# Two moves in a two-layer spectral MLP: GpSimd issues the stores of a matrix's sums, and VectorE adds a seventh product earlier

## The chip, the core and the metric

The kernel runs on one core of a Trainium2 chip. The engines of the core work side by side, each through its own list of instructions in order: TensorE (PE in the profile; PEld is its loading of weights) multiplies into the banks of PSUM, VectorE (DVE) and ScalarE (ACT) work elementwise, GpSimd (POOL) does small elementwise work here, and SyncE (SP; its queue is SPq) issues the transfers between the device's memory and the on-chip memory SBUF. An instruction that waits for a semaphore holds up everything behind it in its engine's list. The metric is the device time of one execution in microseconds; less is better.

## What is computed

Two sublayers, A and B, run in turn, twice, over one sequence of 2048 rows with 512 features, all in float32.

```python
# A: Fourier mixing, the real part of a DFT over rows and features
a = einsum("bsd,ed->bse", x, dft_hid_re);  b = einsum("bsd,ed->bse", x, dft_hid_im)
y = einsum("ts,bse->bte", dft_seq_re, a) - einsum("ts,bse->bte", dft_seq_im, b)
# B: a shift between rows, then an MLP with 1376 hidden features
h  = gelu(layernorm(x) @ w1);  x1 = x + shifted(h) @ w2
out = x1 + gelu(layernorm(x1) @ w3) @ w4
# the whole
x = x + A(layernorm(x));  x = x + B(layernorm(x))     # layer 0
x = x + A(layernorm(x));  x = x + B(layernorm(x))     # layer 1
```

## The kernel before

**Numbers in two parts.** Every operand of a product is split into a high part (a rounded copy, made by ScalarE) and a low part (what the copy lost, made by VectorE). A product is then three matmuls (`mm3`, lines 343 to 345): high by high, high by low, low by high.

**Sublayer A by chunks.** The 2048 output rows are four chunks of 512. In each chunk an x phase (`x_phase`) and a y phase (`y_phase`) multiply the coefficients of the DFT over rows with sums and differences of the input's rows. Each phase runs over eight pairs of row tiles. The x phase accumulates into the PSUM banks psc, psb and psa, the y phase into psc, psd, psb and psa. The coefficients come from memory into the buffers `raw`, and are split into a ring of four slots, `ring0` to `ring3`: VectorE forms a difference (line 285), ScalarE casts it (286), VectorE makes the low part (300). `stream()` hands out the next slot, and before it does, it prepares as many later ones as the ring has room for; so each `stream()` in the code is also a place where VectorE, ScalarE and SyncE get work.

**The product with the hidden DFT matrix.** The 512x512 product of a chunk with the DFT over features is made of seven smaller products of half-sized blocks instead of eight, the seven forms. In layer 1 the x phase of a chunk also multiplies the seven forms of the chunk before it. `HAT7 = (5, 10, 11, 12, 13, 14, 15)` gives the step of the x phase, two to a pair of tiles, at which each form is multiplied (`hid7`, into psd, two banks in turn). One step later VectorE adds its result into the rows X1 or pairs[1] (`hid7_out`, line 520, a `tmp<-tmp,psd` at line 567). The seventh form falls on step 15, the last, so its add has no step behind it: it comes after the last product of the x phase (line 616), behind whatever the last `stream()`, the late work and the hook of step 15 have put into VectorE's list: the low part of a sum of w4's blocks (line 1883), and in chunks 1 and 2 the statistics of two row tiles (lines 377 to 382).

**The right forms.** The seven right-hand blocks of the hidden DFT matrix, each in high and low part, are made once, in layer 0, and kept in memory as `hsd`. That happens beside the last pair of chunks of layer 0's MLP, in four quarters (`hs_forms`, `hs_quarter`): a quarter loads two blocks `hs` of the matrix (lines 1208 and 1211), VectorE forms four sums, and then, in four steps, ScalarE casts (line 1224), VectorE makes the low parts (1229) and the result is stored (1230). Three buffers `hp` (hp0, hp1 and hp2) serve the seven stores of a quarter, so hp1 is used three times and hp0 and hp2 twice. Each step rides with one step of preparing layer 1's input (`bg`), among them the statistics of row tiles, whose power and product run on GpSimd (lines 362 and 363). The MLP's own transfers go through the same queue of SyncE: `w4r` (line 943) and `w3b` (line 958) are the weights of the products that TensorE runs meanwhile. The products of the MLP go through four banks, psa and psd, which VectorE empties by adds named `rest<-rest,psa` and `rest<-rest,psd` (line 567).

The order on each engine is the order in which the Python code issues instructions; no scheduler moves them.

Of the kernel before, what the change touches and what calls it, by code (L numbers as in the profile page):

```python
# [8 lines left out]
F32 = mybir.dt.float32  # L9
# [9 lines left out]
NP = NT // 2  # L19
# [26 lines left out]
def spectral_mlp_kernel(ctx: ExitStack, tc: tile.TileContext, x, ws, hs, w1, w2, w34, out):  # L46
    nc = tc.nc
# [110 lines left out]
    def piece(src, a=0, b=2):  # L158
        pieces.append((src, a, b))
        return len(pieces) - 1  # L160
# [25 lines left out]
    for layer in range(LAYERS):  # L186
        for c in range(NC):
# [15 lines left out]
            for k in range(NP):  # L203
# [4 lines left out]
                p = piece(ws[c, k][:, 2:4])  # L208
# [120 lines left out]
    def stream():  # L329
        i = state["use"]  # L330
        if i and items[i - 1][3] is None:
            state["done"] += 1
        state.update(use=i + 1, over=i)
        prefetch()
        while state["two"] <= i:
            stage_two()
        if items[i][0] == "form":
            return raw_in[place[items[i][1][0]]]
        return slots.pop(i)


    def mm3(o, lh, ll, rh, rl, first, last, more=False):
        nc.tensor.matmul(o, lh, rh, start=first, stop=False, skip_group_check=more)  # L343
        nc.tensor.matmul(o, lh, rl, start=False, stop=False, skip_group_check=more)  # L344
        nc.tensor.matmul(o, ll, rh, start=False, stop=last, skip_group_check=more)  # L345
# [153 lines left out]
    def hid7(n):  # L499
        ps, (lo, _) = PD[n % 2], forms[n]  # L500
        new = n in (0, 1, 3, 6)
        for h in range(2):
            s = stream()
            for i in range(2):
                j = 2 * h + i
                for q in range(2):
                    v = slice(q * P, (q + 1) * P)
                    first = new and not (j or q)
                    o = ps[:, q * DH : (q + 1) * DH]
                    mm3(o, hf[n % 2][:, j, v], lo[:, j, v], s[:, i, 0], s[:, i, 1], first, True, not first)  # L510

    def hid7_out(n):
        ps = PD[n % 2].rearrange("p (t d) -> p t d", t=2)
        x1, x2 = X1, pairs[1]
        if n == 4:
            x2 = x2.rearrange("p t (h d) -> p t h d", h=2)
            add(x2, x2, ps.unsqueeze(2).broadcast_to([P, 2, 2, DH]))
            return
        t, v = ((x1, left), (x2, left), (x1, right), (x2, right), None, (x1, right), (x1, left))[n]
        add(t[:, :, v], t[:, :, v], ps, ALU.subtract if n == 1 else ALU.add)  # L520
# [45 lines left out]
    def add(o, a, b, op=ALU.add):  # L566
        nc.vector.tensor_tensor(o, a, b, op=op)  # L567

    def run_late(*names):
        for i in names:  # L570
            for f in late.pop(i, ()):
                f()

    def x_phase(c, hook, seven=False, tiles=0):
        h = 0
        re0s, re1s, im0s, im1s = by_tile[tiles]
        ready = []

        def form_steps(step):
            if seven and step in HAT7:  # L580
                ready.append(HAT7.index(step))
                hid7(ready[-1])

        def form_outs(step):
            while ready and HAT7[ready[0]] < step:
                hid7_out(ready.pop(0))

        for k in range(NP):
            first, last = k == 0, k == NP - 1
            form_steps(2 * k)  # L590
            while c and not seven and h < NP and HAT[h] == k:
                s = stream()
                ri, dp = HORDER[h % 4]
                hid(ri, dp, s, PD, 2 * (h // 4), h % 4 == 0, h % 4 == 3)
                if h % 4 == 3:
                    at_mix = c == NC - 1 and h > 4
                    add_y(c - 1, h // 4, PD, X1, "10" if at_mix else 2 * k if h < 4 else "y", xs[5] if at_mix else X1)
                h += 1
            s = stream()
            run_late(2 * k)  # L600
            hook(2 * k)
            form_outs(2 * k)
            mm_half(PC, ax[k][:, 2], s[:, 0], first, last)
            mm_half(PB, ax[k][:, 1], s[:, 1], first, last)
            form_steps(2 * k + 1)
            if last:
                for i in range(2):
                    nc.scalar.copy(im1s[:, i], PC[i])  # L608
                for i in range(2):
                    nc.scalar.copy(re1s[:, i], PB[i])  # L610
            s = stream()
            run_late(2 * k + 1)
            hook(2 * k + 1)
            form_outs(2 * k + 1)
            mm_half(PA, ax[k][:, 0], s[:, 0], first, last)
        form_outs(2 * NP)
        for i in range(2):
            nc.scalar.copy(re0s[:, i], PA[i])
# [78 lines left out]
    def hid(ri, dp, s, acc, t0, first, last):  # L697
        for i in range(2):
            for t, a in enumerate(acc):
                w = slice((t0 + t) * P, (t0 + t + 1) * P)  # L700
                mm3(
                    a,
                    rr[ri][dp][:, i, 0, w],
                    rr[ri][dp][:, i, 1, w],
                    s[:, i, 0],
                    s[:, i, 1],
                    first and i == 0,
                    last and i == 1,
                )
# [3 lines left out]
    def add_y(c, half, ps, to, defer, kept=None):  # L713
        j = c * TC + 2 * half
        for i in range(2):
            add(to[:, i], ps[i], to[:, i])
        late.setdefault(defer, []).append(lambda: y_stats(j, to if kept is None else kept))
# [140 lines left out]
    def by_pairs(layer, zs, xin, dst):  # L858
# [344 lines left out]
        def hs_quarter(m, r, fp, places):  # L1203
            b11, b12, b21, b22 = (t[:, :, v] for t in (m, r) for v in (left, right))
            raw = [tf[:, :, 1] for _, tf in fp]

            def load_m():
                nc.sync.dma_start(m, places[0][1])

            def load_r():  # L1210
                nc.sync.dma_start(r, places[0][2])

            def sums():
                add(raw[1], b12, b11, ALU.subtract)
                add(raw[2], b22, b12, ALU.subtract)
                add(raw[0], b22, raw[1], ALU.subtract)
                add(b12, raw[0], b21, ALU.subtract)

            def outs(*which):
                which = [(i, n, raw[i] if src is None else src) for i, n, src in which]  # L1220

                def highs_():
                    for i, _, src in which:
                        act(fp[i][0][:, :, 0], src)

                def lows_():
                    for i, n, src in which:
                        t = fp[i][0]
                        nc.vector.tensor_tensor(t[:, :, 1], src, t[:, :, 0].bitcast(F32), op=ALU.subtract)
                        nc.sync.dma_start(places[n][0].rearrange("p i (l w) -> p i l w", l=2), t.bitcast(F32))  # L1230

                return highs_, lows_

            nothing = lambda: None
            parts = [
                (nothing, sums),
                outs((1, 3, None), (2, 4, None), (0, 2, None)),
                outs((1, 0, b11), (2, 1, b12)),
                outs((0, 6, b21)),
                outs((1, 5, b22)),  # L1240
            ]
            return [(load_m, load_r), *parts]
# [15 lines left out]
        for pair in range(n_pairs):  # L1258
# [62 lines left out]
            for p in range(NF // 2):  # L1321
                prep = {} if kept else w_prep(p)
                u, v, x, y = sets[p % 2]
                w = w3b[(5 * pair + p) % 2]
# [563 lines left out]
    for layer in range(LAYERS):  # L1888
# [4 lines left out]
        for c in range(NC):  # L1893
            if layer == 0 and c == 0:
# [58 lines left out]
                def hook(i):  # L1953
                    k, odd = divmod(i, 2)
                    if not i:
                        second_low(1)
                        xp_stats(1)
                        second_low(0)
                        state["two"] += 1
                        issue_dma()  # L1960
                        state["limit"] = 4
                        prefetch()
                    state["limit"] = w_items[layer]
                    if not odd:
                        if k + 1 < NP:
                            xp_norm(k + 1, 3)
                            xp_main(k + 1)
                        if not k:
                            xp_main_lows(1)
                    else:  # L1970
                        if 0 < k < NP - 1:
                            xp_main_lows(k + 1)
                        if k + 2 < NP:
                            xp_stats(k + 2)
                        if k:
                            xp_sums(k - 1)
                            xp_highs(k - 1, False)
                            xp_lows(k - 1, False)
                    w4_split(i)
# [180 lines left out]
```

## Time and profile before

| | |
|---|---|
| time, median of 3 runs | 1453.88 us (1451.45 to 1456.33) |
| the profiled execution | 1454.98 us |
| its span, first to last instruction | 1452.9 us |
| mean granted clock of TensorE | 0.996 |
| TensorE, VectorE, ScalarE, GpSimd busy | 98%, 83%, 50%, 5% of the span |
| moved by DMA | 325 MB, 224 GB/s on average |

In a timeline row the columns are the start in microseconds, the duration, the engine, the line of the kernel and the operation, output<-inputs with their sizes, and in brackets the idle time of the engine before it with the engine and line that ended it. In a row of waits the numbers are microseconds in total, how many, and the longest. A row of windows gives a stretch, its length, the busy time of PE, PEld, DVE, ACT and POOL with the number of instructions, then the granted TensorE clock, the busy share of the DMA engines and GB/s. Layer 0 ends and layer 1 begins at about 735 us; the chunks of layer 1 whose x phases are spoken of end at about 866, 971 and 1078 us.

### The profile page before, as it was taken

The page shows a single profiled execution, that of the slowest core. Times are in us where ns is not written, and L with a number is a line of the kernel's source. Part 1 is how long each engine was busy: PE and PEld are TensorE (multiplying, and loading weights), DVE is VectorE, ACT ScalarE, POOL GpSimd, SP SyncE. Part 2 cuts the span into 40 slices and gives each one's busy share as a digit, 9 for nine tenths or more (in the row PEclk, how much of TensorE's full clock was granted, in tenths as well). Part 3 has the DMA queues.
Part 4 walks back from the last instruction along what each step waited for, and adds up shares of the span by engine and source line. Part 5 has one row for each costly group of instructions (what it writes and reads, how often), then busy time and mean ns, then how long its engine had stood idle before and what let it go on. Part 6 is the DMA issues. An engine that isn't in the chain of part 4 may idle for free.

```text
span 1452.9 us, 18506 instructions
## 1 busy us (share of the span) xinstructions
PE 1420.9 (98%) x6681; PEld 1188.4 (82%) x6681; DVE 1204.9 (83%) x1725; ACT 731.8 (50%) x1020; POOL 76.6 (5%) x105
## 2 busy tenths in 40 slices
PE   9999999999999999998999989989989999999999
PEld 7888888888888888876888878878878888899887
DVE  7986998989978897667799878879879797897676
ACT  5663554445566654344555443444445666444342
POOL 2100000000002000000000000000000011000000
PEclk9999999999999999999999999999999999999999
DMA  7867657568645758877655577576687537586864
GB/s 247 274 204 234 200 173 261 173 200 296 226 133 161 268 214 282 329 251 263 232 173 190 203 256 225 187 269 222 207 294 240 173 102 275 165 250 217 320 205 163
DMA packets 145628, 325.24 MB, mean 224 GB/s; under 512 B 10624, under 2 KB 61568, under 8 KB 142848
## 3 DMA queue, kind: packets, MB, share of 16 engines
q1 hardware_dynamic: 145536, 324.05, 66.9%
q8 instruction: 53, 0.87, 0.2%
q14 instruction: 39, 0.32, 0.1%
HBM read 262.41 MB, written 61.60 MB: 223 GB/s over the span
## 4 chain that ended last, share of the span: by engine, by line
PE 83%; DVE 9%; DMA 4%; ACT 2%; issue 2%; SPq 0%; DVEq 0%; ACTq 0%
PE psd L343 8%; PE psd L345 8%; PE psd L344 8%; PE psa L343 7%; PE psa L344 7%; PE psa L345 7%; PE psb L344 6%; PE psb L343 6%; PE psb L345 6%; PE psc L344 6%; PE psc L345 6%; PE psc L343 6%; DVE ring L300 1%; DVE rest L567 1%; DMA raw<-in_ws 1%
## 5 line engine op out<-in xcount | busy, mean ns | idle before, releaser
L300 DVE TENSOR_TENSOR ring<-raw,ring 128x1024 fp32r<-128x1024 f32 x102 | 124.2, 1220 | 19.0 <-ACT ring L279 18.7
L279 ACT CAST ring<-raw 128x1024 fp32r<-128x1024 f32 x103 | 107.8, 1051 | 56.3 <-PE psd L345 25.6
L383 POOL TENSOR_TENSOR rs<-ve,mhalf 128x4 f32<-128x4 f32 x16 | 25.0, 1562 | 746.1 <-DVE nm L382 746.1
L343 PE MATMUL psd<-ring,ay 128*128 128x512 f32 x126 | 50.1, 398 | 7.8 <-DVE tmp L567 7.8
L300 DVE TENSOR_TENSOR ring<-ring1f,ring 128x512 fp32r<-128x512 f32 (+1 forms) x56 | 53.3, 952 | 2.9 <-ACT ring L282 2.9
L286 ACT CAST ring<-ring0f 128x1024 fp32r<-128x1024 f32 x28 | 29.5, 1053 | 50.5 <-DVE ring0f L285 50.2
L286 ACT CAST ring<-ring2f 128x1024 fp32r<-128x1024 f32 x28 | 29.6, 1056 | 48.8 <-DVE ring2f L285 48.8
L343 PE MATMUL psd<-rawr,hf 128*128 128x256 f32 x168 | 47.7, 284 | 5.8 <-issue 4.8
L343 PE MATMUL psc<-ring,ay 128*128 128x512 f32 x128 | 50.2, 392 | 2.0 <-ACT rr11f L608 1.7
L300 DVE TENSOR_TENSOR ring<-ring3f,ring 128x1024 fp32r<-128x1024 f32 (+1 forms) x50 | 49.3, 986 | 3.0 <-ACT ring L282 2.6
L362 POOL TENSOR_TENSOR rs<-ve,mhalf 128x2 f32<-128x2 f32 (+2 forms) x33 | 29.2, 886 | 426.6 <-DVE nb L361 407.6
L391 ACT ACTIVATE tmp<-xs,nb,rs 128x512 f32<-128x512 f32 x56 | 43.3, 810 | 15.8 <-POOL nb L363 12.6
L344 PE MATMUL psb<-ring,ay 128*128 128x512 f32 x128 | 50.3, 393 | 0.8 <-DVE ring L300 0.8
L343 PE MATMUL psb<-ring,ay 128*128 128x512 f32 x128 | 50.5, 394 | 0.0
L345 PE MATMUL psb<-ring,ay 128*128 128x512 f32 x128 | 50.1, 391 | 0.0
L345 PE MATMUL psd<-ring,ay 128*128 128x512 f32 x126 | 49.9, 396 | 0.0
L344 PE MATMUL psc<-ring,ay 128*128 128x512 f32 x128 | 49.8, 389 | 0.0
L345 PE MATMUL psc<-ring,ay 128*128 128x512 f32 x128 | 49.8, 389 | 0.0
L344 PE MATMUL psd<-ring,ay 128*128 128x512 f32 x126 | 49.8, 395 | 0.0
L344 PE MATMUL psa<-ring,ay 128*128 128x512 f32 x126 | 49.0, 389 | 0.0
L343 PE MATMUL psa<-ring,ay 128*128 128x512 f32 x126 | 49.0, 389 | 0.0
L345 PE MATMUL psa<-ring,ay 128*128 128x512 f32 x126 | 49.0, 389 | 0.0
(896 smaller groups left out, 4757.8 us busy)
## 6 DMA issues: line engine op xcount, KB each, us to landing
raw<-in_ws SPq DMA_DIRECT2D x183, 512.0 KB, 5.2
w4r<-w4d SPq DMA_DIRECT2D x44, 512.0 KB, 5.3
rawr<-hsd SPq DMA_DIRECT2D x42, 512.0 KB, 4.8
w3b<-w3d SPq DMA_DIRECT2D x10, 1792.0 KB, 9.3
raw<-in_hs SPq DMA_DIRECT2D x32, 512.0 KB, 4.0
w3d<-w3b SPq DMA_DIRECT2D x5, 1792.0 KB, 7.0
hsd<-hp SPq DMA_DIRECT2D x28, 256.0 KB, 2.4
x1d<-tmp SPq DMA_DIRECT2D x12, 512.0 KB, 7.4
```

The source lines that it names most:

```text
L279: nc.scalar.copy(dest[:, a:b, 0], r[0][:, a:b])
L286: nc.scalar.copy(dest[:, :, 0], lo)
L300: nc.vector.tensor_tensor(lo, src, hi.bitcast(F32), op=ALU.subtract)
L343: nc.tensor.matmul(o, lh, rh, start=first, stop=False, skip_group_check=more)
L344: nc.tensor.matmul(o, lh, rl, start=False, stop=False, skip_group_check=more)
L345: nc.tensor.matmul(o, ll, rh, start=False, stop=last, skip_group_check=more)
L362: nc.gpsimd.tensor_tensor(rs[:, :n], ve[:, :n], mhalf[:, 0, :n], op=ALU.pow)
L383: nc.gpsimd.tensor_tensor(rs, ve, mhalf[:, :, :2], op=ALU.pow)
L391: nc.scalar.activation(o, s, AF.Identity, bias=mr[2], scale=mr[1])
L567: nc.vector.tensor_tensor(o, a, b, op=op)
```

## The change

```diff
@@ x_phase, form_steps
             if seven and step in HAT7:
                 ready.append(HAT7.index(step))
                 hid7(ready[-1])
+                if step == 2 * NP - 1:
+                    form_outs(2 * NP)
@@ hs_quarter, lows_
                         nc.vector.tensor_tensor(t[:, :, 1], src, t[:, :, 0].bitcast(F32), op=ALU.subtract)
-                        nc.sync.dma_start(places[n][0].rearrange("p i (l w) -> p i l w", l=2), t.bitcast(F32))
+                        nc.gpsimd.dma_start(places[n][0].rearrange("p i (l w) -> p i l w", l=2), t.bitcast(F32))
```

The first edit calls the adds of the forms that are still open, the sixth and the seventh, right after the seventh form's products have been issued, before the last `stream()` of the x phase. The second issues the 28 stores of the right forms from GpSimd. The changed file has two lines more, so its line 1885 is line 1883 of before, 1232 is 1230, and 945, 960, 1210 and 1213 are 943, 958, 1208 and 1211.

On VectorE, at the end of the x phase of chunk 1 in layer 1, before (psd_287 holds the sixth form and psd_286 the seventh, X1 and pairs[1] are in tmp):

```order
L300 TENSOR_TENSOR ring_204<-ring2f,ring_204 128x2x512
L1883 TENSOR_TENSOR w4sum<-w4sumf,w4sum 128x4x256
L377 BN_STATS st<-tmp 128x6 x2
L379 BN_AGGR mv<-st 128x2 x2
L380 TENSOR_SCALAR ve<-mv 128x2
L381 TENSOR_SCALAR ve<-mv 128x2
L382 TENSOR_SCALAR nm<-mv 128x2
L567 TENSOR_TENSOR tmp<-tmp,psd_287 128x2x256
L567 TENSOR_TENSOR tmp<-tmp,psd_286 128x2x256
L285 TENSOR_TENSOR ring3f<-raw_210,raw_213 128x2x512
```

and now:

```order
L300 TENSOR_TENSOR ring_204<-ring2f,ring_204 128x2x512
L567 TENSOR_TENSOR tmp<-tmp,psd_287 128x2x256
L567 TENSOR_TENSOR tmp<-tmp,psd_286 128x2x256
L1885 TENSOR_TENSOR w4sum<-w4sumf,w4sum 128x4x256
L377 BN_STATS st<-tmp 128x6 x2
L379 BN_AGGR mv<-st 128x2 x2
L380 TENSOR_SCALAR ve<-mv 128x2
L381 TENSOR_SCALAR ve<-mv 128x2
L382 TENSOR_SCALAR nm<-mv 128x2
L285 TENSOR_TENSOR ring3f<-raw_210,raw_213 128x2x512
```

The two adds moved ahead of the low part of w4's sums and of the statistics; the same stands in chunk 2, and in chunk 3 only L1883 lies between. No other engine's order is changed by it.

On SyncE, in the second quarter of the right forms, before:

```order
L1230 DMA hsd_95<-hp_4396 128x512
L1230 DMA hsd_97<-hp_4398 128x512
L1230 DMA hsd_93<-hp_4394 128x512
L1230 DMA hsd_89<-hp_4396 128x512
L1230 DMA hsd_91<-hp_4398 128x512
L943 DMA w4r_251<-w4d_114 128x1024
L1230 DMA hsd_101<-hp_4394 128x512
L1208 DMA hs_4400<-in_hs 128x512
L943 DMA w4r_253<-w4d_115 128x1024
L1230 DMA hsd_99<-hp_4396 128x512
L1211 DMA hs_4401<-in_hs 128x512
L958 DMA w3b_236<-w3d_86 128x3584
```

and now:

```order
L945 DMA w4r_251<-w4d_114 128x1024
L1210 DMA hs_4400<-in_hs 128x512
L945 DMA w4r_253<-w4d_115 128x1024
L1213 DMA hs_4401<-in_hs 128x512
L960 DMA w3b_236<-w3d_86 128x3584
```

The seven stores of the quarter left the queue; the two loads of the next quarter's blocks now wait for VectorE themselves, where the stores ahead of them did so before.

On GpSimd, which had nothing between the statistics of two quarters, the same quarter now reads:

```order
L362 TENSOR_TENSOR rs<-ve,mhalf 128x2
L363 TENSOR_TENSOR nb<-nb,rs 128x2
L1232 DMA hsd_95<-hp_4396 128x512
L1232 DMA hsd_97<-hp_4398 128x512
L1232 DMA hsd_93<-hp_4394 128x512
L1232 DMA hsd_89<-hp_4396 128x512
L1232 DMA hsd_91<-hp_4398 128x512
L1232 DMA hsd_101<-hp_4394 128x512
L1232 DMA hsd_99<-hp_4396 128x512
L362 TENSOR_TENSOR rs<-ve,mhalf 128x2
L363 TENSOR_TENSOR nb<-nb,rs 128x2
```

The seven stores stand between the statistics of their quarter and those of the next.

## The prediction

> **What bounds the kernel now.** I read the page's busy shares first, then the waits of the matmul engine, then the timeline at the places where the two edits stand, and last the granted clock there.
>
> ```profile
> PE 1420.9 (98%) x6681; PEld 1188.4 (82%) x6681; DVE 1204.9 (83%) x1725; ACT 731.8 (50%) x1020; POOL 76.6 (5%) x105
> PE psd L343 <- DVE tmp L567: 7.8, 3, 3.2
> PE psa L343 <- DVE rest L567: 4.3, 3, 3.1
> PE psd L343 <- DVE rest L567: 3.3, 2, 2.7
> ```
>
> TensorE (PE) is busy 98% of the span, so only what it waits for can be won. The other rows are its largest waits on VectorE (DVE): microseconds in total, times, the longest. The first group, three times in layer 1, belongs to the edit of the seventh form; the next two, five times at 642 to 681 us in layer 0, to the edit of the stores.
>
> **The seventh form (layer 1, chunks 1 to 3).** The y phase begins with six matmuls into psc, and then wants psd, which holds the sixth and seventh forms until VectorE has added both into the rows.
>
> ```profile
> 867.41 1.22 DVE L1883 TENSOR_TENSOR w4sum<-w4sumf,w4sum 128x1024 fp32r<-128x1024 f32 x1
> 868.04 0.40 PE L345 MATMUL psc<-ring,ay 128*128 128x512 f32 x1
> 870.29 1.28 DVE L567 TENSOR_TENSOR tmp<-tmp,psd 128x512 f32<-128x512 f32 x2
> 871.49 1.22 DVE L285 TENSOR_TENSOR ring3f<-raw,raw 128x1024 f32<-128x1024 f32 x1
> 871.62 0.80 PE L343 MATMUL psd<-ring,ay 128*128 128x512 f32 x1 [3.19 <-DVE tmp L567]
> 972.28 1.22 DVE L1883 TENSOR_TENSOR w4sum<-w4sumf,w4sum 128x1024 fp32r<-128x1024 f32 x1
> 976.49 0.50 PE L343 MATMUL psd<-ring,ay 128*128 128x512 f32 x1 [3.18 <-DVE tmp L567]
> 1078.83 1.22 DVE L1883 TENSOR_TENSOR w4sum<-w4sumf,w4sum 128x1024 fp32r<-128x1024 f32 x1
> 1081.30 0.50 PE L343 MATMUL psd<-ring,ay 128*128 128x512 f32 x1 [1.45 <-DVE tmp L567]
> ```
>
> The two adds (L567, 1.28 together) stand behind the low part of w4's sums (L1883) and, in chunks 1 and 2, the statistics. By the new order they stand where L1883 stands now. VectorE does the same instructions, so everything from ring3f (871.49) on starts as before, and L1883 with what follows it starts 1.28 later. Chunk 1: adds from 867.41 to 868.69, so psd starts at 868.7 in place of 871.62: 2.9 us. Chunk 2: 972.28 + 1.28 = 973.6 in place of 976.49: 2.9. Chunk 3: 1078.83 + 1.28 = 1080.1 in place of 1081.30: 1.2. Sum 7.0 of the 7.8 waited; the 0.3 us between the last psc matmul (ends about 868.4) and 868.7 stays in each.
>
> ```profile
> 871.60:874.40 2.80, 2.77 (x7) 2.20 (x8) 1.11 (x1) 1.05 (x1) 1.17 (x1) 0.50 0.88 263
> 976.50:978.60 2.10, 2.10 (x6) 1.69 (x7) 1.07 (x1) 0.94 (x1) 1.13 (x1) 0.66 0.87 232
> 978.60:980.40 1.80, 1.80 (x6) 1.37 (x5) 1.50 (x2) 0.29 (x2) 0.00 (x0) 0.50 0.73 266
> 1079.00:1082.00 3.00, 1.55 (x7) 0.99 (x6) 3.00 (x4) 1.58 (x4) 0.00 (x0) 1.00 0.40 164
> ```
>
> The wait has a second price. In these stretches (the number behind the five engines is TensorE's granted clock) the clock is half behind the waits of 3.2 us and full behind the one of 1.45. At half clock 2.8 us do 1.4 us of work; 2.1 us at 0.66 lose 0.7 and 1.8 us at 0.50 lose 0.9. Shorter waits should save these 3.0 us too. This edit: 7.0 + 3.0 = 10.0 us.
>
> What is late next is the ring slot behind the ones already prepared:
>
> ```profile
> 872.80 1.05 ACT L286 CAST ring<-ring3f 128x1024 fp32r<-128x1024 f32 x1 [3.64 <-DVE ring3f L285]
> 874.59 1.23 DVE L285 TENSOR_TENSOR ring0f<-raw,raw 128x1024 f32<-128x1024 f32 x1 [1.88 <-PE psd L345]
> 875.73 1.22 DVE L300 TENSOR_TENSOR ring<-ring3f,ring 128x1024 fp32r<-128x1024 f32 x1
> 880.04 0.39 PE L343 MATMUL psb<-ring,ay 128*128 128x512 f32 x1
> ```
>
> TensorE wants ring3 at 880.04, and 2.9 + 1.4 earlier afterwards, at 875.7 (its low part one matmul later). ring3f and its cast stay; ring0f no longer waits 1.88 for psd and runs right behind ring3f, to about 873.9, and ring3's low part runs 873.9 to 875.1. That is 0.6 us of room, so I cost it at nothing. On SyncE's queue the store of w4's sums waits for L1883, so the coefficient loads behind it issue 1.28 later: between nothing and 1.3 us a chunk. I take nothing, since none of the ring's rows here waits for a load.
>
> **The stores (layer 0, last pair).** In each of four quarters VectorE makes four sums of a block of the DFT matrix, ACT and VectorE split seven blocks through three buffers hp0 to hp2, and SyncE stores each.
>
> ```profile
> 639.01 5.40 SPq L1230 DMA_DIRECT2D hsd<-hp  x5
> 646.66 0.42 SPq L1208 DMA_DIRECT2D hs<-in_hs  x1
> 648.09 0.47 SPq L1211 DMA_DIRECT2D hs<-in_hs  x1
> 653.82 0.43 DVE L567 TENSOR_TENSOR hp12f<-hs 128x256 f32<-128x256 f32 x1 [3.72 <-DMA hsd<-hp]
> 642.23 0.50 PE L343 MATMUL psa<-b,w3b 128*128 128x512 f32 x1 [0.66 <-DVE rest L567]
> 661.48 0.50 PE L343 MATMUL psa<-b,w3b 128*128 128x512 f32 x1 [3.05 <-DVE rest L567]
> 680.33 0.79 PE L343 MATMUL psd<-b,w3b 128*128 128x512 f32 x1 [2.67 <-DVE rest L567]
> 680.30:683.00 2.70, 2.67 (x6) 2.15 (x7) 1.36 (x4) 2.70 (x7) 0.00 (x0) 0.50 0.17 65
> ```
>
> Five stores in order hold SyncE from 639.01 to 644.41, and w4's and the next block's loads queue behind them. So the last store of the quarter travels among these loads, and VectorE, whose next sum overwrites its buffer, stands 3.72 us at 653.82. All that VectorE owes TensorE in that quarter is late by it: 3.05 us at 661.48, and 0.66 and 2.67 in the neighbours, the last with 2.7 us at half clock behind it (1.35 lost). With the stores on GpSimd, w4's load and the first block load (L1208) go out while TensorE still works on earlier tiles, only the second block load (L1211) waits for the quarter's last split, and the last store need not queue behind a w4 load. Then the next sums begin when VectorE comes to them, and 0.66 + 3.05 + 2.67 + 1.35 = 7.7 us go.
>
> What it costs is how long GpSimd takes for a store. No row shows GpSimd issuing a DMA:
>
> ```profile
> L1230 SPq DMA_DIRECT2D hsd<-hp x28: 319/357/411, 619.7 to 685.3; - x28
> DMA to landing us min/median/max: 2.0/2.4/6.0
> L383 POOL TENSOR_TENSOR rs<-ve,mhalf x16: 1007/1760/1985, 125.6 to 1183.1; 128x4 f32<-128x4 f32 x16
> 639.62 0.20 POOL L363 TENSOR_TENSOR nb<-nb,rs 128x2 f32<-128x2 f32 x1
> 658.87 0.20 POOL L363 TENSOR_TENSOR nb<-nb,rs 128x2 f32<-128x2 f32 x1
> 643.16 0.76 DVE L1229 TENSOR_TENSOR hp<-hs,hp 128x256 fp32r<-128x256 f32 x2 [0.99 <-ACT hp L1224]
> 645.67 0.41 ACT L1224 CAST hp<-hs 128x256 fp32r<-128x256 f32 x1 [0.50 <-DMA hsd<-hp]
> 622.48 0.41 ACT L1224 CAST hp<-hs 128x256 fp32r<-128x256 f32 x1 [0.17 <-DMA hsd<-hp]
> 625.16 0.69 DVE L567 TENSOR_TENSOR rest<-rest,psd 128x512 f32<-128x512 f32 x1
> 626.45 0.39 PE L343 MATMUL psd<-b,w3b 128*128 128x512 f32 x1
> ```
>
> The lower end is SyncE's 0.36 us; the upper one 1.99, the longest of GpSimd's own longest instruction. I take 1.0, that instruction's shortest, as the nearest to one uncontended GpSimd instruction, and 2.0 us from the issue's end to landing (2.4 less 0.36). GpSimd does the quarter's statistics first (L363, to 639.82), then three stores back to back; the store behind the split of 643.16 goes 643.6 to 644.6 and lands at 646.6. ACT's cast of the same buffer waits for that, at 645.67 now: 0.95 later, and with it the add that frees a bank. In the first quarter the second store ends at 622.6 and lands at 624.6 in place of 622.48: 2.1 later; the add of 625.16 ends at 628.0 in place of 625.85, and the matmul of 626.45 waits 1.5. The second quarter's 0.95 falls into time that TensorE lost there already; the third's and fourth's count. Cost 1.5 + 2 x 0.95 = 3.4; this edit 3.4 - 7.7 = -4.3 us.
>
> At 0.36 us the cost is about 1.2, so -6.5. Seven stores, a landing and 5.25 us from the sums (653.82) to the end of the statistics (659.07) go round once a quarter, 7g + 7.3, against 18.85 now (661.48 to 680.33). Above g = 1.65 GpSimd sets the pace, and each 0.1 us costs 0.7 a quarter; at g = 1.5 the gain is about eaten by later casts (0), at 1.99 three quarters lose 2.4 each, with the first quarter's casts some +8.
>
> [...]
>
> **Sum.** The profiled execution took 1454.98 us, 1.1 above the median of the runs, 1453.88. 1454.98 - 10.0 - 4.3 = 1440.7, say 1441.
>
> **The rivals.** First, slower: GpSimd takes 2.2 us or more a store. Then a quarter takes over 22.7, 3.9 more than now in three quarters, and with the first quarter's casts the edit costs 14 or more; the whole then stands at or above 1459. It breaks even near g = 2.0. For it: the upper row is 1.99; against it: that row is arithmetic by a power, and the same engine does L363 in 0.20. [...]
>
> Second, the stores win nothing: the second block load, which still waits for the quarter's last split, keeps the sums where they are, or GpSimd needs 1.5. Then 1445.0. For it: that load issued at 648.09 and the sums ran 5.7 later.
>
> Third, the clock drops all the same, since TensorE also waits earlier in those phases: 1441 + 3 = 1444. Against it: chunk 3 waits 1.45 and keeps full clock.
>
> Fourth, ring3 is late after all by its 0.6 of room and more, and two chunks give back 1 to 2 us each: about 1444.
>
> **Numbers.** Forecast 0.50, second rival 0.20, third 0.08, fourth 0.10, slower 0.07; 0.05 for GpSimd between 1.8 and 2.1, about no change. About 0.3%, 4.4 us, is what a measurement tells from no change (the runs spread over 1451.45 to 1456.33). Faster 0.87, same 0.06, slower 0.07. The range goes from 1437 (the stores at -6.5, 1438.5, and 1.5 of the waits that I left in) to 1451 (GpSimd at 1.85 us, where three quarters lose 1.4 each and the edit costs some 6); it holds the second to fourth rivals.
>
> **What would show it.** Right: the matmul into psd waits under 0.5 us in chunks 1 and 2, granted clock 1.00 behind it; the waits on rest at 661 and 680 shrink under 1 us; GpSimd's stores near 1 us each. Wrong: ACT's casts wait over 2 us for hsd in every quarter, VectorE's sums wait longer than 3.7, or GpSimd's statistics come late because stores stand before them.

## The result, and the profile after

The changed kernel took 1459.53 us in the median of 6 runs (1456.33 to 1460.58), the kernel before 1455.01 (6 runs, 1451.45 to 1457.54): a ratio of 1.0035 with a 95% interval of 1.002 to 1.005. It is slower by some 4.5 us where the prediction had it faster by 13. The profiled execution of after took 1460.14 us, its span 1458.3.

The page's busy line, and those of TensorE's waits after that bear on the two edits (microseconds in total, times, the longest):

```profile
PE 1420.9 (97%) x6681; PEld 1187.4 (81%) x6681; DVE 1204.2 (83%) x1725; ACT 732.1 (50%) x1020; POOL 93.1 (6%) x133
PE psd L343 <- DVE rest L567: 9.0, 4, 3.6
PE psa L343 <- DVE rest L567: 8.4, 4, 3.6
PE psb L344 <- DVE ring L300: 2.2, 1, 2.2
PE psc L343 <- ACT imLf L610: 1.7, 2, 1.0
PE psd L343 <- DVE tmp L567: 0.9, 3, 0.3
```

The last row is the seventh form, 0.9 us now where it was 7.8. The first two are the stores' place in layer 0: 17.4 us of waits on `rest`, where the kernel before had 7.6. Two smaller groups grew as well, the ring (2.2, before 0.8) and the first matmul of a y phase on ScalarE's copy `imLf` (1.7, before 0.2).

TensorE runs the same 6681 matmuls in the same order in both kernels, so the start of a matmul here less its start before tells how far after lies behind at that point. Three rows of TensorE's timeline in layer 0 and the three of the seventh form, all of after:

```profile
626.98 0.50 PE L343 MATMUL psd<-b,w3b 128*128 128x512 f32 x1 [1.41 <-DVE rest L567]
646.70 0.66 PE L343 MATMUL psa<-b,w3b 128*128 128x512 f32 x1 [3.61 <-DVE rest L567]
691.48 0.80 PE L343 MATMUL psd<-b,w3b 128*128 128x512 f32 x1 [3.60 <-DVE rest L567]
881.06 0.50 PE L343 MATMUL psd<-ring,ay 128*128 128x512 f32 x1 [0.32 <-DVE tmp L567]
982.15 0.50 PE L343 MATMUL psd<-ring,ay 128*128 128x512 f32 x1 [0.30 <-DVE tmp L567]
1084.24 0.50 PE L343 MATMUL psd<-ring,ay 128*128 128x512 f32 x1 [0.32 <-DVE tmp L567]
```

Just ahead of the first one, after was 1.0 us early. Then it is 0.5 late (626.98 against 626.45), 4.5 late (646.70 against 642.23) and 11.2 (691.48 against 680.33); at the end of layer 0 it is 11.5. So layer 0 lost 12.5 us, and only the stores' edit stands there. In layer 1 it is 9.4 late at the first of the psd rows, 5.7 at the second, 2.9 at the third: the adds win. At the end it is 5.1 late, so 2.1 were lost again behind the third row. The whole is 1.0 ahead, 12.5 lost in layer 0, 10.0 won at and behind the three psd matmuls, 1.4 lost just ahead of the first two of them, at psc (`imLf`), and 2.1 at the ring.

What holds VectorE up in layer 0, as rows of after's timeline, with the loads and the store concerned; the last three rows are those of the source view of the seventh stores of the first three quarters (issue to landing):

```profile
639.22 0.43 DVE L567 TENSOR_TENSOR hp11f<-hs 128x256 f32<-128x256 f32 x1 [5.79 <-issue]
660.60 0.42 DVE L567 TENSOR_TENSOR hp12f<-hs 128x256 f32<-128x256 f32 x1 [3.24 <-issue]
684.00 0.42 DVE L567 TENSOR_TENSOR hp13f<-hs 128x256 f32<-128x256 f32 x1 [6.14 <-issue]
630.34 0.54 POOL L1232 DMA_DIRECT2D hsd<-hp  x1 [0.40 <-DVE hp L1231]
630.38 0.41 SPq L960 DMA_DIRECT2D w3b<-w3d  x1
652.99 0.40 ACT L1226 CAST hp<-hs 128x256 fp32r<-128x256 f32 x1 [3.26 <-DMA hsd<-hp]
DMA to landing us min/median/max: 8.5/8.5/8.5
DMA to landing us min/median/max: 6.3/6.3/6.3
DMA to landing us min/median/max: 9.2/9.2/9.2
```

The seventh store of the first quarter is issued by GpSimd at 630.34 and lands 8.5 later, at 638.8; VectorE's first sum of the next quarter, which overwrites that store's buffer, starts 0.4 behind it. ("issue" stands in the bracket because the profile names no releaser there.) The three waits are 15.2 us together, where before they were 9.4 (2.38, 3.72, 3.25). The store itself took 8.5, 6.3 and 9.2 us, where before it took 4.7, 6.0 and 5.6. SyncE issues the load of `w3b`, 1792 KB, 0.04 us behind that store's start. ScalarE's casts wait as well, 3.26 us in the second quarter. The queues in two stretches behind it (packets, MB, share of the DMA engines), first 632 to 634.5 us, then 634.5 to 638.8:

```profile
q1 hardware_dynamic: 107, 0.83, 105.1%
...
q1 hardware_dynamic: 92, 1.09, 63.1%
q0 software_dynamic: 80, 0.26, 15.0%
```

q1 is SyncE's queue, q0 GpSimd's. (A share can pass 100% because a packet counts whole in the stretch where it starts.) In the first 2.5 us nothing of the store moves, only loads; then all of its 256 KB crawl between pieces of `w3b`: from 636.2 to 637.6 us 32 packets of the store, 0.13 MB, start beside 33 of `w3b`'s, 0.47 MB. So both queues take shares of the DMA engines in one stretch, 63.1% and 15.0%. Why the store's packets wait through the 2.5 us ahead of it is not shown.

### The profile page after: what moved, and what is told of

Its sections match the earlier page's. It is cut to its first block, busy times and chain, and to the rows that moved or that the text cites. A ratio compares the mean times of both kernels' runs of the same rounds, so it can differ in the third digit from the quotient of the medians.

```text
span 1458.3 us, 18509 instructions
## 1 busy us (share of the span) xinstructions
PE 1420.9 (97%) x6681; PEld 1187.4 (81%) x6681; DVE 1204.2 (83%) x1725; ACT 732.1 (50%) x1020; POOL 93.1 (6%) x133
## 4 chain that ended last, share of the span: by engine, by line
PE 78%; DVE 11%; DMA 4%; issue 4%; ACT 3%; POOL 0%; SPq 0%; DVEq 0%; ACTq 0%; POOLq 0%
PE psd L343 8%; PE psd L345 8%; PE psd L344 8%; PE psa L343 6%; PE psa L345 6%; PE psa L344 6%; PE psb L344 6%; PE psb L345 6%; PE psb L343 6%; PE psc L344 6%; PE psc L345 6%; PE psc L343 6%; DVE ring L300 2%; DMA raw<-in_ws 1%; DMA hsd<-hp 1%
```

## The experiments

**The stores alone.** (In the diffs from here on, three dots stand for code that is left out of a line.)

```diff
-                        nc.sync.dma_start(places[n][0]..., t.bitcast(F32))
+                        nc.gpsimd.dma_start(places[n][0]..., t.bitcast(F32))
```

> Only the stores move to GpSimd; the adds stand where they stood. Matmul by matmul the changed kernel fell 12.5 us behind between 626 and 692 us. Theory: that is all the stores' doing, because the seventh store of a quarter now shares the DMA engines with w3b's 1792 KB instead of standing ahead of it in one queue. About 1467 us (+12); VectorE's sums wait 3 to 6 us in each later quarter, and a seventh store lands 6 us or more behind its issue. Rival, the prediction's sum: -4.3, 1450.7, and the loss would lie with the adds. Second rival, the stores win nothing: 1455.

Measured: 1468.01 us, ratio 1.0088 (1.0067 to 1.0108), 13 us slower. The first sums of the second and of the last quarter, in its timeline:

```profile
639.43 0.43 DVE L567 TENSOR_TENSOR hp11f<-hs 128x256 f32<-128x256 f32 x1 [5.81 <-issue]
683.48 0.43 DVE L567 TENSOR_TENSOR hp13f<-hs 128x256 f32<-128x256 f32 x1 [5.55 <-issue]
```

The seventh stores land 8.5, 6.5 and 8.6 us behind their issue. The loss is all the stores', and the prediction's -4.3 is out by 17 us. By the starts of the matmuls, 12.3 of the 13 us are lost in layer 0.

**The adds alone.**

```diff
                 hid7(ready[-1])
+                if step == 2 * NP - 1:
+                    form_outs(2 * NP)
```

> Only the adds move; SyncE keeps the stores. Theory, from the changed kernel's trace: psd waits 0.3 us in place of 3.2, 3.2 and 1.5, the clock stays full behind it, -3.9, -3.9 and -1.1, and then ring slots come 2.1 late in chunk 3: -6.5 to -8, about 1448. Rival, the prediction's sum without that loss: -10, 1445. Rival, the gain needs the earlier delay of layer 0 (other transfers beside the chunks): under -3, 1452 or more.

Measured: 1447.46 us, ratio 0.9948 (0.9927 to 0.9968), 7.5 us faster. With the 13 us of the stores that makes +5.6, where both edits together measured +4.5. The wait on the ring in chunk 3 is there, 2.2 us. Where it comes from is read at ScalarE's wait for the store of rows `x1d`, whose buffer `tmp` it overwrites. First three rows of the kernel before, then the same three of this one:

```profile
1080.13 0.33 SPq L1886 DMA_DIRECT2D w4s<-w4sum  x1
1083.29 0.72 SPq L239 DMA_DIRECT2D x1d<-tmp  x1
1091.31 1.52 ACT L391 ACTIVATE tmp<-xs,nb,rs 128x512 f32<-128x512 f32 x2 [3.23 <-DMA x1d<-tmp]
```

```profile
1074.30 0.33 SPq L1888 DMA_DIRECT2D w4s<-w4sum  x1
1077.20 0.70 SPq L239 DMA_DIRECT2D x1d<-tmp  x1
1085.17 1.52 ACT L391 ACTIVATE tmp<-xs,nb,rs 128x512 f32<-128x512 f32 x2 [5.12 <-DMA x1d<-tmp]
```

The chunk's psd matmul starts at 1081.30 before and at 1073.15 here. Against that, the store of w4's sums goes out 2.3 us later than before (1.15 behind it, where it was 1.17 ahead), the row store 2.1 later and ScalarE's activation 2.0 later. Behind the activation in ScalarE's list stand the casts of `ring2` and `ring3`. VectorE's low part of `ring2` waits for the first of them (2.80 us here, 1.14 before), the low part of `ring3` follows it in VectorE's list, and that is what TensorE waits for.

The traced execution is the slowest of its six (1450.29). Its clock stood at 0.50 for 3 us behind that wait of 2.19 us, which cost some 1.6 us more; behind the same wait in the kernel after, 2.17 us, it stayed at 1.00; the mean granted clock was 0.995 in the one execution and 0.998 in the other. So the price of the late ring differs between executions by what the clock does.

**The adds, with the store of w4's sums on GpSimd.**

```diff
-            nc.sync.dma_start(w4s[k], w4_sum.bitcast(F32))
+            nc.gpsimd.dma_start(w4s[k], w4_sum.bitcast(F32))
```

> Adds early, stores of the right forms on SyncE, and the stores of w4's sums (the line behind L1883) on GpSimd, so that the coefficient loads behind them in SyncE's queue no longer wait for L1883. Theory (the 2.1 us lost at 1096 to 1100 us come from coefficient loads that the later store of w4's sums holds up): no wait on ring there, 2 us faster than the adds alone, about 1446. Rival (the ring is late because of VectorE's own order): the waits on ring stay 1.5 us or more and the time equals that of the adds alone, 1448.

Measured: 1448.95 us, ratio 0.9958 (0.9945 to 0.9971), no better than the adds alone. The wait on the ring and what leads to it:

```profile
PE psb L344 <- DVE ring L300: 2.1, 1, 2.1
1074.74 0.62 POOL L1888 DMA_DIRECT2D w4s<-w4sum  x1 [86.04 <-DVE w4sum L1885]
1076.12 1.31 SPq L239 DMA_DIRECT2D x1d<-tmp  x1
1084.63 1.52 ACT L391 ACTIVATE tmp<-xs,nb,rs 128x512 f32<-128x512 f32 x2 [4.71 <-DMA x1d<-tmp]
```

The psd matmul starts at 1073.02 here, so the row store goes out 0.95 us sooner against TensorE than with the adds alone, but ScalarE's activation comes only 0.4 sooner. The late ring costs 1.6 us of TensorE's time up to the psb matmul, where with the adds alone it cost 2.0. Taking the store out of SyncE's queue does not take its 1024 KB off the DMA engines: from the row store's issue to the activation that waits for it pass 8.5 us here, and 8.0 with the adds alone. My theory that the order of issue alone costs the 2 us falls; that the later transfers of this place do is left, and the next run asks for it.

**The adds in chunks 1 and 2 alone.**

```diff
                 hid7(ready[-1])
+                if step == 2 * NP - 1 and c < NC - 1:
+                    form_outs(2 * NP)
```

> The adds stand early in chunks 1 and 2 of layer 1 alone; chunk 3 and all stores are as before. Theory: in chunk 3 the early adds win 1.1 us at psd, but the store of w4's sums starts later against TensorE, the row store (x1d) behind it lands later, ScalarE waits for it and ring comes 2 us late; without the edit there, psd waits 1.5 again and the ring 0.8 as before: -8 to -9 against before, 1446.5, and no 2 us wait on ring. Rival (the late ring of chunk 3 follows from the earlier chunks, since all of TensorE's work comes sooner against transfers of fixed length): the 2 us on ring stay and psd waits 1.5 besides, -6, 1449.

Measured: 1446.31 us, ratio 0.9941 (0.9928 to 0.9955), 9 us faster than before. Its waits:

```profile
PE psd L343 <- DVE tmp L567: 1.7, 2, 1.4
PE psc L343 <- ACT imLf L610: 1.6, 1, 1.6
PE psb L344 <- DVE ring L300: 0.6, 1, 0.6
```

psd waits 1.4 us again in chunk 3, and the ring 0.6 (before 0.8). So it is chunk 3's own early adds that bring the late ring: there the edit wins 1.1 and loses 2.1. The median is below those of both runs before it, but the intervals overlap, so that step of 1 us is read from the traces, not from the times. That the loss belongs to chunk 3's own adds is what this run shows; the way through the row store is read from the rows of three traces, and no run moved that store alone.

**The seventh store of a quarter on SyncE, the other six on GpSimd, adds as before.**

```diff
-                        nc.sync.dma_start(places[n][0]..., t.bitcast(F32))
+                        (nc.sync if n == 5 else nc.gpsimd).dma_start(places[n][0]..., t.bitcast(F32))
```

> Adds as before; GpSimd issues six stores of a quarter, SyncE the seventh, which so stands ahead of the next block's second load and of w3b in one queue again. Theory (sharing with w3b): the seventh lands about 2 to 3 us behind its issue, VectorE's sums begin within 1 us of the second load's landing, and most of the loss goes: 1455 to 1459, what is left being casts that wait for stores beside the w4 load. [...]

Measured: 1457.88 us, ratio 1.0027 (1.0012 to 1.0042): of the 13 us that the stores cost, 10 are gone with one store in seven. Its sums' waits, from the timeline:

```profile
634.79 0.42 DVE L567 TENSOR_TENSOR hp21f<-hs,hs 128x256 f32<-128x256 f32 x1 [0.53 <-DMA hs<-in_hs]
654.33 0.43 DVE L567 TENSOR_TENSOR hp22f<-hs,hs 128x256 f32<-128x256 f32 x1 [1.31 <-DMA hs<-in_hs]
672.56 0.43 DVE L567 TENSOR_TENSOR hp23f<-hs,hs 128x256 f32<-128x256 f32 x1 [1.04 <-DMA hs<-in_hs]
647.88 0.40 ACT L1224 CAST hp<-hs 128x256 fp32r<-128x256 f32 x1 [2.37 <-DMA hsd<-hp]
```

The seventh store lands 2.7, 3.7 and 3.3 us behind its issue, and what the sums wait for now is the second block load (`hs<-in_hs`), as the prediction's second rival had it. The last row is most of what remains of the loss in layer 0: ScalarE's casts wait 2.37, 2.08 and 1.85 us for a store of GpSimd's, in two quarters the fourth, which travels beside w4's and the block's loads. The first quarter's 1.4 us at its first matmul stay too. GpSimd's own issue, 0.54 us a store, isn't what cost the 10 us: it still issues six of the seven.

**The seventh store on ScalarE's queue.**

```diff
-                        nc.sync.dma_start(places[n][0]..., t.bitcast(F32))
+                        (nc.scalar if n == 5 else nc.gpsimd).dma_start(places[n][0]..., t.bitcast(F32))
```

> Adds as before; GpSimd issues six stores of a quarter, ScalarE's queue the seventh. Theory 1 (any queue of its own shares the DMA engines with w3b's large pieces): the seventh lands 6 us or more behind its issue, VectorE's sums wait 3 to 6 us, 1463 to 1470. [...]

Measured: 1459.07 us, ratio 1.0027 (1.0012 to 1.0043). The seventh stores, one by one, in the source view (engine, duration in ns, start), and the sum that waited longest:

```profile
L1230 ACTq DMA_DIRECT2D hsd<-hp x1: 364/364/364, 630.0 to 630.0; - x1
DMA to landing us min/median/max: 3.8/3.8/3.8
L1230 ACTq DMA_DIRECT2D hsd<-hp x1: 362/362/362, 648.4 to 648.4; - x1
DMA to landing us min/median/max: 5.4/5.4/5.4
L1230 ACTq DMA_DIRECT2D hsd<-hp x1: 362/362/362, 667.7 to 667.7; - x1
DMA to landing us min/median/max: 9.3/9.3/9.3
677.09 0.43 DVE L567 TENSOR_TENSOR hp13f<-hs 128x256 f32<-128x256 f32 x1 [5.94 <-DMA hsd<-hp]
```

Theory 1, with 6 us or more to landing, holds in one quarter of the three. ScalarE's queue can do as badly as GpSimd's (9.3 us, and here the profile names the store as the releaser), so it isn't GpSimd; but it can also do well (3.8). The three differ in what SyncE's queue still had under way when the store was issued: the load of w4 issued ahead of it had landed 1.0 us earlier in the first case, and landed 1.4 and 3.0 us later in the other two. That fits a store that stands behind what the other queue has already handed over, but it was not tried apart, and it does not order the landings on GpSimd's queue: in the kernel after, w4's load had landed 1.4 us before the store that took 8.5, 0.1 before the one that took 6.3, and landed 2.3 behind the start of the one that took 9.2.

**The load of w3b in seven pieces, all stores on GpSimd.**

```diff
-                nc.sync.dma_start(w3b[i].bitcast(F32), w3d[n % (NF // 2)])
+                if layer:
+                    nc.sync.dma_start(w3b[i].bitcast(F32), w3d[n % (NF // 2)])
+                    return
+                to, src = (t.rearrange("p l k w -> p (l k w)") for t in (w3b[i].bitcast(F32), w3d[n % (NF // 2)]))
+                for u in range(0, 14 * 2 * P, CH):
+                    nc.sync.dma_start(to[:, u : u + CH], src[:, u : u + CH])
```

> Adds as before, all stores on GpSimd, and layer 0's loads of w3b cut into seven of 256 KB, so that their pieces are 2 KB a partition and no longer 14 KB. Theory (the DMA engines take the two queues' pieces in turn, and a store's 4 KB wait for 14 KB each time): the seventh store lands within 4 us of its issue, the sums wait 2 to 3 us less a quarter, 1457 to 1461. Rival (the store stands behind all that SyncE's queue has already handed over, whatever its pieces): it lands 7 us or more behind its issue as before, 1466 or more.

Measured: 1461.07 us, ratio 1.0046 (1.0028 to 1.0064), 5.6 us slower than before, where the stores alone cost 13. The landings of the seventh stores in three quarters, one of the sums, and one of ScalarE's casts:

```profile
DMA to landing us min/median/max: 4.8/4.8/4.8
DMA to landing us min/median/max: 4.7/4.7/4.7
DMA to landing us min/median/max: 5.0/5.0/5.0
635.48 0.43 DVE L567 TENSOR_TENSOR hp11f<-hs 128x256 f32<-128x256 f32 x1 [1.82 <-issue]
649.22 0.40 ACT L1229 CAST hp<-hs 128x256 fp32r<-128x256 f32 x1 [3.13 <-DMA hsd<-hp]
```

The store is issued where it was, beside the same 1792 KB, and lands in 4.7 to 5.0 us instead of 6.5 to 8.6. So what held it was how that load is handed over, and not that GpSimd issues the store. Splitting the load changes two things at once, the size of the pieces and their time: the seven issues now start between 630.57 and 633.77. Which of the two frees the store, this run does not tell. I had expected under 4 us, and what the rest is stays open.

The sums now wait 1.82, 1.66 and 1.93 us, less than in the kernel before, and yet 5.6 us are lost. The last row shows where: ScalarE's casts wait 3.13, 2.08 and 1.28 us for GpSimd's stores beside w4's load, as in the run with the seventh store on SyncE, while the kernel before had some 0.5 us there in each quarter.

**Two chunks' adds, and w4's loads one step later in layer 0.**

```diff
                     w4_part(acc1, f, h, lambda: at_point(4 + i))
-                    w4_load()
+                    if not next_too:
+                        w4_load()
                     one()
+                    if next_too:
+                        w4_load()
```

> Adds early in chunks 1 and 2, all stores on SyncE, and in layer 0's last pair each load of w4 goes out behind the step of the right forms that it stood ahead of, so that one 512 KB load fewer travels ahead of a quarter's seventh store and of the next block's second load. Theory (what VectorE's sums wait for is how long the transfers ahead of these two take): the sums begin about 1.3 us sooner in three quarters, 512 KB at some 400 GB/s, -3 to -4 beside the adds of two chunks alone, 1443. Rival (the loads of w4 then come late for TensorE's products, or SyncE waits for VectorE ahead of them): new waits of TensorE on w4r take the gain or more, 1446 to 1452.

Measured: 1444.27 us, ratio 0.9937 (0.9917 to 0.9956). No wait on w4's loads appears. By the starts of the matmuls layer 0 gains 1.9 us on the run with two chunks' adds, half of what I expected: the sums begin 1.9, 1.0 and 1.9 us sooner, but the waits on `rest` fall only from 7.1 to 5.4. In the times the two aren't apart, since the intervals overlap. It is the lowest median of this study.

## Why the prediction was wrong

**The seventh form, right to the size.** Forecast -10.0 at the place: 7.0 from the waits, 3.0 from the clock. The waits fell from 7.8 to 0.9, 6.9 us. The clock, in the stretches behind the psd matmuls of after:

```profile
880.50:883.50 3.00, 2.68 (x13) 2.03 (x12) 3.00 (x6) 0.97 (x2) 0.00 (x0) 1.00 0.20 85
982.00:984.00 2.00, 1.85 (x8) 1.55 (x9) 2.00 (x4) 0.56 (x2) 0.00 (x0) 1.00 0.00 0
646.70:649.50 2.80, 2.80 (x7) 2.23 (x8) 1.47 (x4) 2.79 (x7) 0.99 (x2) 0.53 0.38 146
```

It is 1.00 where it was 0.50 and 0.66. Behind the psd matmuls of chunks 1 and 2 after gains another 1.5 and 1.6 us on before, which is the clock's part. So 6.9 + 3.1 = 10.0. The third rival (the clock drops anyway) is out at these places. What the clock does behind a wait is not settled by its length alone in these traces: in the kernel before, 3.05 us at 661.48 left it at 1.00 and 2.67 at 680.33 halved it. So the 3.0 were priced from what one execution showed, and not by a rule. The third row is layer 0: behind its new wait of 3.61 us the clock drops to 0.53, which adds to the stores' cost.

**What was costed at nothing behind the adds.** The step was: the coefficient loads behind the store of w4's sums issue 1.28 us later, "between nothing and 1.3 us a chunk", taken as nothing because no row of the ring waits for a load. In chunk 3 it was 2.1 us. I had followed the loads in that queue but not the row store behind them, whose landing ScalarE waits for ahead of the ring's casts; the 3.23 us that ScalarE already waited there before were in the trace and not in my argument. It isn't the fourth rival either: the slot `ring3` that stands behind psd, at 880.04 before, was not late in any chunk. The adds in two chunks leave the loss out.

**The stores, wrong in sign.** The step that failed is "0.66 + 3.05 + 2.67 + 1.35 = 7.7 us go": that the seventh store, once out of SyncE's queue, "need not queue behind a w4 load", and the sums start when VectorE comes to them. In SyncE's queue the store stood behind w4's load and ahead of `w3b`; on GpSimd's it stood ahead of nothing, and w3b's load was issued 0.01 to 0.29 us behind it. I priced what it leaves behind and not what it comes to travel with. In its place: sums that wait 15.2 us instead of 9.4, ScalarE's casts behind stores that share with loads (3.26 us at 652.99, where I had 0.95 more than 0.50), 17.4 us of waits on `rest` instead of 7.6, and a granted clock of 0.53 behind the longest. Sending the seventh store by SyncE takes 10 of the 13 us back, cutting w3b's load some 7.5. Most of what is left are the casts, the term that the prediction put at 0.95 us in each of two quarters.

**GpSimd's price, wrong in the harmless direction.** The stores in after, in the source view (ns; first and last start):

```profile
L1232 POOL DMA_DIRECT2D hsd<-hp x28: 542/542/747, 620.1 to 696.9; - x28
DMA to landing us min/median/max: 2.3/2.7/9.2
```

I took 1.0 us, it is 0.54 (the first one 0.75), and the sixteen stores that had no load under way beside them landed in 2.3 to 2.7, near the 3.0 I had. With 0.54 my sum would have been about -6, further off. (The terms of that sum also give 0.9 at 0.36 us, where it says about 1.2, and 5.4 at 1.5 us, where it says that the gain of 7.7 is about eaten; neither changes the outcome.) So the slower rival, 2.2 us a store, did not come about: it named the right sign for a reason that the runs exclude. The first quarter's later casts are the one part that came as costed: 1.5 forecast, 1.41 waited at 626.98. That is luck in part: the two issues took 1.30 us where I had 2.0, but GpSimd began them some 0.6 us later against TensorE than I had it.

**The second rival** (the block load keeps the sums where they are) is what holds once the seventh store is out of the way: there the sums wait 0.5 to 1.3 us for that load. So even with an undisturbed seventh store, only a part of the 7.7 could have been won.

**What stays open.** The first psc matmul of a y phase waits up to 1.6 us for ScalarE's copy `imLf`, which stands behind the cast of a ring slot whose load lands late. In chunk 1 this stands ahead of the moved adds; yet it came out 1.2 us later with the adds alone and 0.4 earlier with the stores alone. It moves by a microsecond or so from kernel to kernel, and I have no cause that the runs show.

## What to carry to other kernels

A transfer that is moved to another engine's queue leaves the wait in front of it and also its place ahead of everything behind it: list what it will share the DMA engines with from then on, above all large loads issued within its flight, and who waits for its landing. Here one short store whose buffer the next step overwrites did better in the queue of the large loads, ahead of the largest (2.7, 3.7 and 3.3 us to landing, against 8.5, 6.5 and 8.6 with all seven on GpSimd). And when work is put later on one engine to bring other work forward, follow its queue to the end: the cost, 2.1 us in chunk 3, came through a store that stands behind the loads that I had looked at.

## What the runs showed of the hardware

A store of 256 KB from GpSimd that landed in 2.3 to 2.7 us where no load was under way beside it (16 of the 28 in after) took 6.3 to 9.2 beside a 1792 KB load issued within 0.3 us of it from another queue, and in the first of these cases moved nothing in a stretch of 2.5 us in which the other queue worked; with the same load cut into pieces of 256 KB it took 4.7 to 5.0. GpSimd's issue of a store takes 0.54 us in the median, and the longest of the 28 took 0.75, with VectorE busy 83% of the span. Waits of TensorE of 2.17 and 2.19 us in the same place left its granted clock at 1.00 in one execution (after) and at 0.50 in another (the adds alone), and waits of 2.67 and 3.05 us in one execution (before) left it at 0.50 behind the shorter and at 1.00 behind the longer.
